# Attention followed by a two-layer feed-forward on one core: the last four loads of v made to wait for an output transpose

## The chip, the cores and the metric

One core of a Trainium2 chip runs the whole kernel. The metric is the device time of one execution in microseconds (us), as a median over runs. The engines are named as the profile names them: PE is TensorE, PEld its weight load, DVE is VectorE, ACT is ScalarE, POOL is GpSimd and SP is SyncE. SPq and POOLq stand for transfers that SP and GpSimd start.

## The reference

```python
def _attn_ref(q, k, v, bias_table):            # q, k, v: 8 batches x 8 heads x 576 x 64
    scores = np.matmul(q, k.transpose(0, 1, 3, 2)) / np.sqrt(D)
    scores = scores + bias[None]               # a bias by distance and head, from 32 buckets
    attn = np.exp(scores - scores.max(-1, keepdims=True))
    attn = attn / (attn.sum(-1, keepdims=True) + 1e-09)
    return np.matmul(attn, v)

def reference(...):
    x = attn_out.transpose(0, 2, 1, 3).reshape(B * S, H * D)   # 4608 x 512
    h = x @ w_in                                                # 512 x 2048
    return np.maximum(0.01 * h, h) @ w_out                      # 2048 x 512
```

## The kernel before

**Attention** runs over 32 pairs of heads: pair n is heads 2p and 2p+1 of batch b, with b = n // 4 and p = n % 4. For each pair the rows of q and k are copied from the loaded tiles `qn` and `kn` into a tile `pr` (L435, DVE), turned by a DMA transpose on SP (`tu<-pr`, L440), and copied into `qt` and `kt` (L466). Scores go to `ps_s` (L492 to L500), the exponentials to `at` (L506 to L513), the bias is multiplied in as a factor (L526), and the product with v goes to `ps_o` and `ps_om` (L547 from the tile `v4`, shown as `v`, and L562 from `vn`). DVE divides by the sums (L574, L575) into `opair`. A DMA transpose on SP (`xT<-opair`, L581) then puts the pair's output into `xT[p]`, where channels are rows and tokens are columns. `xT[p]` is a ring of four batches, 576 columns each, with 64 columns behind the last. One such transpose writes 640 columns, five blocks of 128: the 576 tokens of its batch, and 64 columns past them that carry nothing.

**The feed-forward** takes tiles T of 512 tokens. Its first product reads `xT[0]` to `xT[3]` in turn (L614, later in blocks L671), so a tile can't be finished before the fourth pair of the batch that holds its last token is turned. Its second product is L744, and DVE adds up the results in `y` (L760), which SP stores. The matmuls of the feed-forward stand between those of the attention on the same in-order PE.

**Loads.** v, q and k are loaded by GpSimd, since they change type on the way, in order on one queue. There are two buffers of each, so the load of batch b goes where batch b-2 was. For each b from 2 on, `plan_loads` (L956) queues two loads each for q and k and then `load_v_part` three times (L299): four transfers of `vn` (L302) and two of `v4` (L308). Before its first transfer GpSimd waits until PE has made the last product that reads the old `vn`, that of the fourth pair of batch b-2. Behind the six transfers of v(b) stand on the same queue the four of q and k of batch b+1 (L294), of which the first two serve the first two pairs of that batch.

**The order** of every engine is set before the program runs, by the class `Plan`, which simulates the engines with costs, ranks and tables. In it the load of v for b > 3 is already placed behind the output transpose of the fourth pair of batch b-2 (`avs + xt[...]`, L963). That places the load in the plan alone: the program has no wait of its own for it.

Of the kernel before, what the change touches and what calls it, by code (L numbers as in the profile page):

```python
# [79 lines left out]
class Plan:  # L80
# [32 lines left out]
    def add(self, engine, cost, after, go, rank, take=(), give=(), tail=0.0, at=None):  # L113
        t = {"engine": engine, "cost": cost, "after": list(after), "go": go, "rank": rank, "n": len(self.tasks),
             "take": list(take), "give": list(give), "tail": tail, "end": at, "start": at}
        if at is None:
            self.tasks.append(t)
        return t
# [95 lines left out]
def kernel(  # L214
# [10 lines left out]
    nc = tc.nc  # L225

    B, H, S, D = q.shape
# [5 lines left out]
    n_pairs = H // 2  # L233
# [24 lines left out]
    RING = 4  # L258
    RT = RING * S
    xT = [per.tile([P, RT + P - SL], BF16, name=f"xT{p}") for p in range(n_pairs)]  # L260
# [29 lines left out]
    def load_qk(b, h0, h1, js=(0, 1)):  # L290
        i = b % NBUF
        for j in js:
            src, dst = ((q, qn[i]), (k, kn[i]))[j]
            nc.gpsimd.dma_start(  # L294
                out=dst[0:RQ, h0:h1, :, :].rearrange("r h c d -> r h (c d)"),
                in_=src[b, h0:h1, :, :].rearrange("h (r c) d -> r h (c d)", c=NC),
            )

    def load_v_part(b, j):  # L299
        i = b % NBUF  # L300
        for c in ((0,), (1, 2), (3,))[j]:
            nc.gpsimd.dma_start(  # L302
                out=vn[i][:, c, :, 0:D],
                in_=v[b, :, c * P : (c + 1) * P, :].rearrange("h s d -> s h d"),
            )
        if j == 2:
            for e in range(2):
                nc.gpsimd.dma_start(  # L308
                    out=v4[i][e * SL : (e + 1) * SL, :, e, 0:D],
                    in_=v[b, e::2, NJ * P : S, :].rearrange("h s d -> s h d"),  # L310
                )

    def clear_v(eng, i):
        eng.memset(v4[i], 0.0)
        for e in range(2):
            eng.memset(v4[i][e * SL : (e + 1) * SL, :, e, D : D + 1], 1.0)
        eng.memset(vn[i][:, :, :, D : D + 1], 1.0)
# [452 lines left out]
    rowt, cut, sct, ext, avt, nrt, nmt, xt, vt = {}, {}, {}, {}, {}, {}, {}, {}, {}  # L770
# [19 lines left out]
    def moves(t, work, lane, lead, least, yields=0.39):  # L790
        t["moves"], t["lane"], t["lead"], t["least"], t["yields"] = work, lane, lead, least, yields
        return t

    def pool_load(key, cost, go, work, after=(), rank=1):
        t = add("POOL", cost, prev + list(after), go, rank)
        moves(t, work, 0, min(cost + 1.0, 3.2), cost + 2.2, 0.39 if key[0] in ("qk", "v") else 0.2)
        prev[:] = [t]
        L[key] = t
        return t
# [5 lines left out]
    prev.append(clears[0])  # L805
    pool_load(("qk", 0, 2), 1.4, lambda: load_qk(0, 6, H), 2.0, rank=-9)
    pool_load(("v", 0), 5.2, lambda: [load_v_part(0, j) for j in range(3)], 5.5, rank=-8)
    vt[0] = L["v", 0]
    edges = add("POOL", 1.0, list(prev), lambda: [clear_edges(nc.gpsimd, i) for i in range(3)], -7)
    pool_load(("qk", 1, 0), 1.4, lambda: load_qk(1, 0, 4), 2.6, rank=-4)  # L810
    pool_load(("w_in", 0), 0.8, lambda: load_w_in(0), WH, rank=-4)
    clears.append(add("POOL", 1.2, list(prev), lambda: clear_v(nc.gpsimd, 1), -3))
    prev.append(clears[1])
    vt[1] = pool_load(("v", 1), 5.2, lambda: [load_v_part(1, j) for j in range(3)], VB, rank=-2)
    pool_load(("qk", 1, 1), 1.4, lambda: load_qk(1, 4, H), 2.7, rank=-1)
    pool_load(("w_in", 1), 0.8, lambda: load_w_in(1), WH, rank=6)
# [139 lines left out]
    def plan_loads(b):  # L956
        i = n_pairs * (b - 2)
        for hh in range(2):
            ps = [rowt[i + 2 * hh + x][r] for x in range(2) for r in range(2)]
            pool_load(("qk", b, hh), 1.5, lambda hh=hh: load_qk(b, 4 * hh, 4 * hh + 4), 3.0, ps, 10 * i + 500)  # L960
        avs = [t for p in range(n_pairs) for t in avt[i + p]]
        if b > 3:
            avs = avs + xt[i + n_pairs - 1]  # L963
        vt[b] = pool_load(("v", b), 5.0, lambda: [load_v_part(b, j) for j in range(3)], 5.0, avs, 10 * i + 500)

    oin, ins = {}, {}

# [107 lines left out]
    for n in range(N):  # L1075
        if n >= 2 * n_pairs and n % n_pairs == 0:
            plan_loads(n // n_pairs)
        plan_rows(n)
        if n == 0:
            plan_table()  # L1080
            clears[1]["after"].append(hk4t[1])
        plan_pair(n)
# [47 lines left out]
```

## Time and profile before

| | |
|---|---|
| median of 3 runs | 360.85 us (359.72 to 361.23) |
| the profiled execution | 361.39 us |
| its span, first to last instruction | 359.5 us |
| clock granted to TensorE | 1.0 throughout |
| busy share of the span | PE 98%, DVE 81%, ACT 76%, POOL 19% |

The page of the profile gives busy times by engine and by line, the waits name who held up an engine and how long, the timeline lists instructions by start and duration in us, and the chain is the work that ended last, followed backwards. "To landing" is the time from the issue of a transfer until its data is there. A matmul's end is modelled, so that neighbouring matmuls overlap on paper.

### The profile page before, as it was taken

How to read it: one execution, taken by the hardware profiler on the slowest of the kernel's cores; microseconds unless marked ns; L12 is line 12 of the kernel's file. 1: busy time of each engine (PE TensorE's matmuls, PEld its weight loads, DVE VectorE, ACT ScalarE, POOL GpSimd, SP SyncE). 2: the span in 40 equal slices, each digit the busy share in tenths (PEclk: the TensorE clock that was granted, in tenths of full speed). 3: DMA queues.
4: the chain of work that ended last, by engine and by line, in shares of the span. 5: the costliest groups of instructions: out<-in, count | busy, mean ns of one | idle time of the engine just before them, and what ended most of it. 6: DMA issues, size and time to landing. Idle time of an engine off the chain costs nothing.

```text
span 359.5 us, 10118 instructions
## 1 busy us (share of the span) xinstructions
PE 351.3 (98%) x4204; PEld 256.4 (71%) x4204; DVE 292.8 (81%) x703; ACT 274.4 (76%) x365; POOL 69.3 (19%) x107
## 2 busy tenths in 40 slices
PE   8999999989999999999999999999999999999996
PEld 6666457746577456745677787657888888888885
DVE  6888899785799649976799899999977669578594
ACT  6997998697898899789878788897746656655630
POOL 8956123070005300800260050000000000000000
PEclk9999999999999999999999999999999999999999
DMA  8999999999538993995599999221220011011022
GB/s 125 157 186 194 209 186 110 148 169 190 130 82 96 202 135 83 126 191 66 88 149 139 175 130 130 82 39 47 60 68 2 31 58 61 2 58 60 31 84 93
DMA packets 106941, 39.31 MB, mean 109 GB/s; under 512 B 82320, under 2 KB 105872, under 8 KB 106896
## 3 DMA queue, kind: packets, MB, share of 16 engines
q0 software_dynamic: 53424, 18.21, 49.9%
q1 hardware_dynamic: 53120, 20.03, 31.9%
q8 instruction: 33, 0.54, 0.7%
q10 hardware_dynamic: 352, 0.43, 0.4%
q14 instruction: 12, 0.10, 0.1%
HBM read 36.70 MB, written 9.44 MB: 128 GB/s over the span
## 4 chain that ended last, share of the span: by engine, by line
PE 64%; DMA 14%; DVE 13%; POOL 4%; issue 2%; ACT 1%; DVEq 0%; ACTq 0%; POOLq 0%
PE pm L744 23%; PE pm L614 15%; PE pm L671 12%; PE ps_s L492 5%; DMA w_out_sb<-in_moe_w_out_dram 4%; DMA tu<-pr 4%; PE ps_om L562 3%; DMA xT<-opair 3%; DMA vn<-in_v_dram 3%; PE ps_o L562 3%; DVE sum L712 3%; DVE at L526 3%; DVE opair L575 2%; POOL vn L302 1%; DVE y L760 1%
## 5 line engine op out<-in xcount | busy, mean ns | idle before, releaser
L506 ACT ACTIVATE at<-ps_s 128x1024 bf16<-128x1024 f32 x124 | 120.7, 1033 | 21.2 <-PE ps_s L492 20.4
L614 PE MATMUL pm<-xT,w_in_sb 128*128 128x512 bf16 (+1 forms) x416 | 85.9, 347 | 1.4 <-DMA xT<-opair 1.0
L526 DVE TENSOR_TENSOR at<-at,hk 128x768 bf16<-128x768 bf16 (+4 forms) x156 | 65.7, 448 | 11.5 <-ACT at L506 9.1
L744 PEld LDWEIGHTS <-gt 128*128 128x128 bf16 x576 | 54.4, 98 | 11.7 <-issue 3.4
L614 PEld LDWEIGHTS <-w_in_sb 128*128 128x128 bf16 x416 | 37.7, 98 | 34.1 <-issue 7.1
L690 ACT ACTIVATE gt<-pm 128x512 bf16<-128x512 f32 x88 | 50.9, 627 | 10.4 <-PE pm L614 10.2
L760 DVE TENSOR_TENSOR y<-pm,y 128x512 f32<-128x512 f32 (+1 forms) x53 | 41.1, 776 | 16.1 <-PE pm L744 14.4
L302 POOL DMA_DIRECT2D vn<-in_v_dram x32 | 28.5, 903 | 131.4 <-PE ps_o L562 119.5
L744 PEld LDWEIGHTS <-sum 128*128 128x128 bf16 x432 | 41.2, 98 | 8.1 <-issue 2.1
L562 PEld LDWEIGHTS <-at 128*128 128x128 bf16 x1240 | 41.1, 98 | 2.8 <-issue 0.7
L492 PE MATMUL ps_s<-qt,kt 64*128 64x512 bf16 x256 | 40.0, 382 | 0.2
L744 PE MATMUL pm<-w_out_sb,gt 128*128 128x256 bf16 x288 | 37.9, 273 | 0.0
L744 PE MATMUL pm<-mix,gt 128*128 128x256 bf16 x288 | 36.7, 273 | 0.0
L744 PE MATMUL pm<-w_out_sb,sum 128*128 128x256 bf16 x288 | 36.0, 273 | 0.0
L681 DVE TENSOR_TENSOR at<-pm,at 128x512 f32<-128x512 f32 (+1 forms) x22 | 18.9, 880 | 9.3 <-ACT at L675 7.2
L675 ACT COPY at<-pm 128x1024 f32<-128x1024 f32 x15 | 15.1, 1009 | 13.8 <-PE pm L671 13.8
L562 PE MATMUL ps_o<-vn,at 128*128 128x65 bf16 x640 | 25.2, 193 | 0.1
L562 PE MATMUL ps_om<-vn,at 128*128 128x65 bf16 x600 | 24.1, 194 | 0.0
L513 ACT ACTIVATE at<-ps_s 128x576 bf16<-128x576 f32 x31 | 20.9, 675 | 0.7 <-PE ps_s L500 0.6
L492 PEld LDWEIGHTS <-kt 64*128 64x128 bf16 x256 | 8.2, 94 | 17.4 <-issue 15.3
L508 ACT ACTIVATE at<-ps_s 128x512 bf16<-128x512 f32 x31 | 19.2, 619 | 0.2
L687 ACT ACTIVATE gt<-at 128x1024 bf16<-128x1024 f32 x15 | 15.9, 1057 | 4.0 <-DVE at L681 4.0
(120 smaller groups left out, 526.7 us busy)
## 6 DMA issues: line engine op xcount, KB each, us to landing
out_dram<-y SPq DMA_DIRECT2D x35, 256.0 KB, 2.2
vn<-in_v_dram POOLq DMA_DIRECT2D x32, 128.0 KB, 6.1
qn<-in_q_dram POOLq DMA_DIRECT2D x14, 288.0 KB, 9.9
kn<-in_k_dram POOLq DMA_DIRECT2D x14, 288.0 KB, 11.3
w_in_sb<-in_moe_w_in_dram POOLq DMA_DIRECT2D x2, 1024.0 KB, 11.5
w_out_sb<-in_moe_w_out_dram POOLq DMA_DIRECT2D x2, 1024.0 KB, 17.4
qn<-in_q_dram POOLq DMA_DIRECT2D x4, 144.0 KB, 4.0
v<-in_v_dram POOLq DMA_DIRECT2D x16, 32.0 KB, 6.2
```

The costliest lines, as they stand in the source:

```text
L302: nc.gpsimd.dma_start(out=vn[i][:, c, :, 0:D], in_=v[b, :, c * P : (c + 1) * P, :].rearrange("h s d -> s h d"),)
L492: nc.tensor.matmul(ps[:, e, :], lhsT=kt[r, u * P : (u + 1) * P], rhs=qt[r, 0:512], start=True, stop=True)
L506: nc.scalar.activation(at[:, :, u, 0:512], ps, AF.Exp, scale=scale)
L508: nc.scalar.activation(at[:, :, :, 512:S].rearrange("p e c i -> p c e i"), ps[:, 0, :].rearrange("p (c e i) -> p c e i", e=2, i=SL), AF.Ex ...
L513: nc.scalar.activation(at4[:, 0:S], ps.rearrange("p e i -> p (e i)")[:, 0:S], AF.Exp, scale=scale)
L526: nc.vector.tensor_tensor(out=o, in0=o, in1=m, op=ALU.mult)
L562: nc.tensor.matmul(ps[:, ic, :], lhsT=at[:, o : o + P], rhs=vn[i][:, c, 2 * p + e, :], start=whole and c == 0, stop=not whole and ic == NJ ...
L614: nc.tensor.matmul(pms[T, f][:, o : o + n], lhsT=w_in_sb[:, c, f * P : (f + 1) * P], rhs=xT[c][:, x : x + n], start=(c == 0 and i == 0), s ...
L671: nc.tensor.matmul(ps[:, i, :], lhsT=w, rhs=x, start=fresh and i % 2 == 0 and c == 0, stop=i % 2 == 1 and c == 1, skip_group_check=not fresh)
L690: nc.scalar.activation(gts[T][:, f, :], pms.pop((T, f)), AF.Prelu, bias=0.0, scale=1.0, alpha=0.01)
L744: nc.tensor.matmul(ps[:, ts, :], lhsT=l[:, ts * P : (ts + 1) * P], rhs=r, start=(ts == 0 or apart) and j == 0, stop=(ts == 1 or apart) and ...
L760: nc.vector.tensor_tensor(out=out_, in0=ps, in1=x, op=ALU.add)
```

## The change

For the loads of v for b = 4, 5, 6 and 7, GpSimd first writes a zero into one element of `xT[3]`: row 0, and the first of the 64 columns past batch b-2. The transpose of the fourth pair of batch b-2 writes that column too, so GpSimd has to wait until that transpose has landed. The six transfers of v follow on the same queue.

```diff
+
+    def behind_x(b):
+        o = (b - 2) % RING * S + S
+        nc.gpsimd.memset(xT[n_pairs - 1][0:1, o : o + 1], 0.0)
...
-        vt[b] = pool_load(("v", b), 5.0, lambda: [load_v_part(b, j) for j in range(3)], 5.0, avs, 10 * i + 500)
+        vt[b] = pool_load(("v", b), 5.0, lambda: [behind_x(b) if b > 3 else None, [load_v_part(b, j) for j in range(3)]], 5.0, avs, 10 * i + 500)
```

No instruction of PE, ACT, DVE or SP changes its place. On GpSimd one memset is added ahead of each of the four loads. The first two pieces below stand around the first of these loads, that for b = 4. The first is GpSimd's queue before. `vn_95` and `v_0_97` are the buffers of v, DMASW a semaphore of GpSimd's transfers and DMAHW one of SP's.

```order
L294 DMA kn_93<-in_k_dram 96x4x384 [waits DMASW2_49,DVE_49]
L302 DMA vn_95<-in_v_dram 128x8x64 [waits DMASW3_49,PE_49]
L302 DMA vn_95<-in_v_dram 128x8x64 [waits DMASW4_49,PE_49]
L302 DMA vn_95<-in_v_dram 128x8x64 [waits DMASW5_49,PE_49]
L302 DMA vn_95<-in_v_dram 128x8x64 [waits DMASW6_49,PE_49]
L308 DMA v_0_97<-in_v_dram 64x4x64 [waits DMASW7_49]
L308 DMA v_0_97<-in_v_dram 64x4x64 [waits DMASW0_49]
L294 DMA qn_92<-in_q_dram 96x4x384 [waits DMASW1_49,DVE_49]
```

The same place of GpSimd's queue in the changed kernel; `xT_81` is `xT[3]`.

```order
L294 DMA kn_93<-in_k_dram 96x4x384 [waits DMASW2_49,DVE_49]
L315 MEMSET xT_81 1x1 [waits DMAHW5_49]
L302 DMA vn_95<-in_v_dram 128x8x64 [waits DMASW3_49,PE_49]
L302 DMA vn_95<-in_v_dram 128x8x64 [waits DMASW4_49,PE_49]
L302 DMA vn_95<-in_v_dram 128x8x64 [waits DMASW5_49,PE_49]
L302 DMA vn_95<-in_v_dram 128x8x64 [waits DMASW6_49,PE_49]
L308 DMA v_0_97<-in_v_dram 64x4x64 [waits DMASW7_49]
L308 DMA v_0_97<-in_v_dram 64x4x64 [waits DMASW0_49]
L294 DMA qn_92<-in_q_dram 96x4x384 [waits DMASW1_49,DVE_49]
```

The memset stands ahead of all six transfers and waits for a transfer of SP; everything behind it on the queue follows it. The next output transpose into `xT[3]`, that of pair 15 a batch later, stands so in SP's queue before (L581):

```order
L581 DMA_TRANSPOSE xT_80<-opair 128x5x128 [waits DMAHW5_49,DVE_49]
L440 DMA_TRANSPOSE tu_110<-pr_107 128x12x96 [waits DMAHW6_49,DVE_49]
L440 DMA_TRANSPOSE tu_108<-pr_105 128x12x96 [waits DMAHW0_49,DMAHW7_49,DVE_49,Activation_49]
L581 DMA_TRANSPOSE xT_81<-opair 128x5x128 [waits DVE_49]
L764 DMA out_dram<-y 128x2x256 [waits DMAHW1_49,DVE_49]
```

And so in the changed kernel, where line numbers are four higher:

```order
L585 DMA_TRANSPOSE xT_80<-opair 128x5x128 [waits DMAHW5_49,DVE_49]
L444 DMA_TRANSPOSE tu_110<-pr_107 128x12x96 [waits DMAHW6_49,DVE_49]
L444 DMA_TRANSPOSE tu_108<-pr_105 128x12x96 [waits DMAHW0_49,DMAHW7_49,DVE_49,Activation_49]
L585 DMA_TRANSPOSE xT_81<-opair 128x5x128 [waits DVE_49,Pool_49]
L768 DMA out_dram<-y 128x2x256 [waits DMAHW1_49,DVE_49]
```

SP's instructions keep their places; only the wait for the memset (`Pool_49`) is new.

## The prediction, on record before the changed kernel ran

> **What bounds the kernel now.** The page comes first, for the busy shares, then the waits of PE, since PE is busy nearly throughout.
>
> ```profile
> PE 351.3 (98%) x4204; PEld 256.4 (71%) x4204; DVE 292.8 (81%) x703; ACT 274.4 (76%) x365; POOL 69.3 (19%) x107
> ```
>
> ```profile
> PE pm L614 <- DMA xT<-opair: 1.0, 2, 0.6
> ```
>
> PE is the bound. The second row says how often PE stood still for an output transpose: twice, 1.0 us in all. That is the first yardstick for a change that only frees output transposes. The chain of waits seems to promise more:
>
> ```profile
> 112.73 5.43 DMA xT<-opair
> ...
> 146.96 6.28 DMA xT<-opair
> ```
>
> These are the transposes of pairs 11 and 15, the last of their batches, with the time from issue to landing (second column). The answer on the tile xT has the range for all 24 output transposes (min, median, max):
>
> ```profile
> DMA to landing us min/median/max: 2.6/4.1/14.5
> ```
>
> So both took over twice the shortest. The windows say what PE lost meanwhile (columns: stretch, its length, PE busy):
>
> ```profile
> 111.60:120.00 8.40, 7.80 (x101) 5.18 (x98) 6.79 (x16) 6.06 (x8) 8.14 (x10) 1.00 1.52 150
> ...
> 144.00:156.00 12.00, 11.57 (x136) 7.45 (x133) 11.75 (x33) 9.05 (x13) 7.46 (x10) 1.00 1.54 152
> ```
>
> PE lacks 0.60 us of the first and 0.43 us of the second stretch. The rest of the 5.43 and 6.28 us was covered by other matmuls. The timeline shows the two places, and that a load of v started just ahead of each transpose:
>
> ```profile
> 111.60 3.54 POOL L302 DMA_DIRECT2D vn<-in_v_dram  x4 [32.77 <-PE ps_o L562]
> ...
> 112.73 1.20 SPq L581 DMA_TRANSPOSE xT<-opair  x1
> ...
> 117.23 0.38 PE L614 MATMUL pm<-xT,w_in_sb 128*128 128x512 bf16 x1
> ...
> 118.21 1.24 PE L614 MATMUL pm<-xT,w_in_sb 128*128 128x512 bf16 x5 [0.60 <-DMA xT<-opair]
> ...
> 144.56 3.52 POOL L302 DMA_DIRECT2D vn<-in_v_dram  x4 [24.82 <-PE ps_o L562]
> ...
> 151.61 1.24 PE L614 MATMUL pm<-xT,w_in_sb 128*128 128x512 bf16 x5
> ...
> 153.28 0.38 PE L614 MATMUL pm<-xT,w_in_sb 128*128 128x512 bf16 x1 [0.43 <-DMA xT<-opair]
> ```
>
> **What goes.** The idle column gives 0.60 + 0.43 = 1.03 us. It counts from the modelled end of the matmul before. Counted from start to start, the five matmuls at 151.61 stand (1.24 - 0.38) / 4 = 0.215 us apart. By that pace the matmul at 118.21 would have started at 117.23 + 0.215 = 117.45, which is 0.76 us earlier, and that at 153.28 at 151.61 + 5 x 0.215 = 152.69, 0.59 us earlier. That is 1.35 us. I take 1.2, between the two.
>
> For the stalls to go whole, the transposes must land within 117.45 - 112.73 = 4.72 us and 152.69 - 146.96 = 5.73 us. The median of 4.1, which includes many transposes beside loads, does that; the 2.6 us of the shortest does it easily. So I take both stalls as gone. What is then late next is PE itself, whose matmuls follow one another.
>
> The other two loads have no such stall to give back:
>
> ```profile
> 177.72 3.65 POOL L302 DMA_DIRECT2D vn<-in_v_dram  x4 [25.70 <-PE ps_o L562]
> 178.56 1.23 SPq L581 DMA_TRANSPOSE xT<-opair  x1
> 208.56 3.53 POOL L302 DMA_DIRECT2D vn<-in_v_dram  x4 [22.98 <-PE ps_o L562]
> 209.37 1.29 SPq L581 DMA_TRANSPOSE xT<-opair  x1
> ```
>
> The waits of PE name only the first two places, so nothing is counted for pairs 19 and 23.
>
> **What is added.** Four memsets of one element. The nearest row, GpSimd's small memset, is 0.10 us; the largest that GpSimd makes is 0.60:
>
> ```profile
> 0.24 0.10 POOL L1114 MEMSET const-float32-0.0<- 128x1 f32 x1 [0.24 <-issue]
> ...
> 5.10 0.60 POOL L314 MEMSET v<- 128x520 bf16 x1
> ```
>
> I take 0.10; even 4 x 0.60 = 2.4 us lies on GpSimd, which waits 23 to 33 us ahead of each of these loads (the bracket of the rows above). The waits that the memset gives to later instructions, those of SP and of the DVE instructions that read `xT[3]`, are over long before: the memset at about 116 is followed by the next transpose into `xT[3]` at 146.96.
>
> **What moves.** The start of each load moves from the release by PE to the landing of the transpose. With 2.6 to 4.1 us to landing and 0.1 for the memset, the loads start at 115.4 to 116.9 instead of 111.60, at 149.7 to 151.2 instead of 144.56, at 181.3 to 182.8 instead of 177.72, and at 212.1 to 213.6 instead of 208.56: some 3.5 to 6.6 us later. Behind each stand the loads of q and k on the queue, later by as much. Who waits for them?
>
> v(4) is first used by the product of pair 16, at 149.91, and its last parts were issued at 115.09 and take 6.2 us by the page's median:
>
> ```profile
> 149.91 0.19 PE L547 MATMUL ps_o<-v,at 64*128 64x65 bf16 x1
> ...
> 115.09 1.29 POOL L308 DMA_DIRECT2D v<-in_v_dram  x2
> ```
>
> ```profile
> v<-in_v_dram POOLq DMA_DIRECT2D x16, 32.0 KB, 6.2
> ```
>
> They landed near 123, with 27 us to spare: nothing. The nearest user of the later q and k is at the third place, where the copies for pair 28 need the first loads of batch 7:
>
> ```profile
> 183.58 0.68 POOL L294 DMA_DIRECT2D kn<-in_k_dram  x1
> ...
> 200.12 0.35 DVE L435 COPY pr<-kn 96x768 bf16<-96x768 bf16 x1
> ...
> 203.94 0.69 DVE L760 TENSOR_TENSOR y<-pm,y 128x512 f32<-128x512 f32 x1 [0.81 <-PE pm L744]
> ```
>
> The answers on transfers at 183.58 and 184.90 have these loads of k with their time to landing:
>
> ```profile
> kn<-in_k_dram POOLq DMA_DIRECT2D x1, 288.0 KB, 12.8
> ...
> kn<-in_k_dram POOLq DMA_DIRECT2D x1, 288.0 KB, 16.6
> ```
>
> So k landed at 183.58 + 12.8 = 196.4, and DVE copied it at 200.12: 3.7 us to spare against 3.6 to 5.1 us of delay at this place. At the worst DVE waits 5.1 - 3.7 = 1.4 us, of which the 0.81 us that it idles at 203.94 takes back some; at the best nothing, since the transfers that no longer share the engines with the transpose also go faster. I take 0.2 us. Moving a transfer doesn't shrink it: SP's next transposes (one at 118.21, one at 183.37) share the engines with the load as before, only with a later part of it. Their results are used long after:
>
> ```profile
> 118.21 2.36 SPq L440 DMA_TRANSPOSE tu<-pr  x1
> ...
> 141.65 1.22 ACT L466 COPY kt<-tu 128x576 bf16<-128x576 bf16 x1
> ```
>
> The transpose of 118.21, for pair 18, is copied at 141.65, and pair 17's stands between, so a few us more cost nothing.
>
> **The sum.** The profiled execution took 361.39 us, 1.9 of it around the span of 359.5. Less 1.2, plus 0.2: 360.4. The median is 0.54 below that execution, so the forecast is 360.85 - 1.0 = 359.85 us.
>
> **The rivals.**
>
> *k comes late (slower).* If the first load of k at the third place takes not 12.8 but, as the second one did, 16.6 us, and starts 4.5 us later, it lands 8.3 us later: DVE waits 8.3 - 3.7 = 4.6 us, 0.8 of it in the gap at 203.94. That costs 3.8, less the 1.2 gained: 363.4 us. It turns slower where DVE's wait exceeds 0.8 + 1.2 = 2.0 us, that is, where k is delayed by more than 5.7 us. For it: DMA traffic is heaviest here. Against it: the delay by the rows ends at 5.1. The Trainium skill's page "DMA: Bandwidth & Descriptors", section "Rules for kernel authors", speaks against the change in general: issue a transfer early and wait for it late, so that its fixed cost overlaps with compute. This place, with its 3.7 us, is the only one found where the rows let that rule cost anything.
>
> *No gain.* The transposes could be slow because of SP's own queue: the transpose at 110.18 ahead, stores from 114.30 behind. Then they land as before, the loads only start later, and the time stays 360.85. For it:
>
> ```profile
> 110.18 1.29 SPq L440 DMA_TRANSPOSE tu<-pr  x1
> ...
> 114.30 2.70 SPq L764 DMA_DIRECT2D out_dram<-y  x2
> ```
>
> Against it: at the second place the only store near comes at 148.63, 1.7 us behind the transpose, which was the slower of the two.
>
> *Copies beside GpSimd's issues.* Three copies into `pr` took twice as long as the rest while GpSimd issued a load of v (start, duration):
>
> ```profile
> 179.67 0.35 DVE L435 COPY pr<-qn 96x768 bf16<-96x768 bf16 x1
> 179.94 0.72 DVE L435 COPY pr<-kn 96x768 bf16<-96x768 bf16 x1
> ...
> 210.69 0.71 DVE L435 COPY pr<-kn 96x768 bf16<-96x768 bf16 x1
> 211.58 0.69 DVE L435 COPY pr<-qn 96x768 bf16<-96x768 bf16 x1
> ```
>
> The moved loads leave these copies alone, 3 x 0.35 = 1.05 us of DVE. With the 1.35 us of the stalls at their fullest the time is 360.85 - 2.4 = 358.45. Against it: DVE isn't the bound. The other way round, up to four copies (those at 150.50, 150.77, 154.53 and 154.80) fall into the moved load of the second place; were all doubled and on the path, 360.85 - 1.2 + 1.4 = 361.05. The Trainium skill's page "SBUF — State Buffer", section "Who interferes with whom", has a rule for this: VectorE copies in a two-port mode and GpSimd share a port pair under an exclusive lock, and the later one blocks. It would make the cost real; the doubled rows agree, and this pair of rivals stands for it.
>
> ```profile
> 150.50 0.35 DVE L435 COPY pr<-qn 96x768 bf16<-96x768 bf16 x1
> ```
>
> This one ran while GpSimd issued loads of q and k (149.27 to 152) and was not doubled.
>
> *The chain is right.* If what the chain credits to the two transposes beyond 2 x 2.6 us came off, it would be 5.43 + 6.28 - 5.2 = 6.5 us: 354.3. PE's 7.80 busy of 8.40 us speaks against it.
>
> **How the numbers follow.** Forecast 0.57 (359.3 to 360.5); no gain 0.15; copies freed 0.12; copies newly hit 0.06; k late 0.07; the chain 0.03. The range leaves out the chain and the late k, and ends at 358.4, the freed copies, and at 361.4, the no-gain case with the half us by which medians and single runs differ here: 0.85 or a little more is inside, less some for what I overlooked. About 0.5% (1.8 us) is what a measurement of this kernel can tell from no change. Faster than 359.05: the chain, most of the freed copies, a little of the forecast, 0.16. Slower than 362.65: most of the late k, 0.05. The rest, 0.79, is within.
>
> **What would show it.** Right: PE no longer waits for xT at either place, both transposes land within 4.7 and 5.7 us, each load of v starts behind the landing, and DVE copies k for pair 28 without idling. Wrong: the transposes take 5 us or more with the load held back (no gain), an idle time of DVE ahead of the copies near 200 that ends with a load of k (late k), or a time outside 358.4 to 361.4 with those rows unchanged.

## The result, and the profile after

| | before | changed |
|---|---|---|
| median, 22 runs each | 361.78 us | 360.31 us |
| ratio, 95% interval | | 0.9948 (0.9926 to 0.9971) |
| the profiled execution, its span | 361.39, 359.5 us | 360.92, 359.2 us |

The change makes the kernel faster by 0.5%: 361.78 x 0.0052 = 1.9 us, with an interval of 1.0 to 2.7 us. The ratio leaves out one slow run of the changed kernel, of 366.03 us, and the two medians, over all runs, differ by 1.47 us. The median of before over 22 runs is 0.9 us above that of the three runs that the prediction had.

The waits of PE in the changed kernel hold no wait for an output transpose any more; these are all five rows (columns: us in total, times, the longest). The first row is a wait in the first 20 us, for the first load of v, where the two programs are the same.

```profile
PE ps_o L566 <- DMA vn<-in_v_dram: 1.2, 2, 0.9
PE ps_w L1099 <- DVE junk L331: 1.1, 1, 1.1
PE ps_tx L593 <- DVE opair L579: 0.4, 2, 0.2
PE pm L618 <- DVE opair L579: 0.2, 1, 0.2
PE ps_u L389 <- DVE hk L392: 0.2, 1, 0.2
```

The timeline of the changed kernel at the two places (start, duration; line numbers are four higher than before):

```profile
113.69 1.20 SPq L585 DMA_TRANSPOSE xT<-opair  x1
116.32 0.09 POOL L315 MEMSET xT<- 1x1 bf16 x1 [34.69 <-DMA xT<-opair]
116.83 3.67 POOL L302 DMA_DIRECT2D vn<-in_v_dram  x4 [0.41 <-PE ps_s L496]
117.53 0.59 PE L618 MATMUL pm<-xT,w_in_sb 128*128 128x512 bf16 x2
118.19 1.46 PE L618 MATMUL pm<-xT,w_in_sb 128*128 128x512 bf16 x6
...
147.22 1.20 SPq L585 DMA_TRANSPOSE xT<-opair  x1
149.84 0.09 POOL L315 MEMSET xT<- 1x1 bf16 x1 [24.83 <-DMA xT<-opair]
150.34 3.54 POOL L302 DMA_DIRECT2D vn<-in_v_dram  x4 [0.41 <-PE ps_s L496]
151.82 1.46 PE L618 MATMUL pm<-xT,w_in_sb 128*128 128x512 bf16 x6
```

Each memset starts within 0.1 us of the landing of the transpose (113.69 + 2.58 = 116.27), the load starts 0.4 us after the memset's end, and the six matmuls that read `xT` run without a gap. The answers on xT at 113.69, 147.22, 178.19 and 209.08 have the same landing time for all four transposes:

```profile
DMA to landing us min/median/max: 2.6/2.6/2.6
```

That is as short as the shortest of before, where the two that PE waited for took 5.4 and 6.3 us.

**A yardstick without the start.** The whole spans compare badly, since the first 66 us of the changed kernel's trace ran up to 2.9 us behind that of before, on the same instructions. PE waited 0.9 us for v there (18.59 us), and the granted clock was 0.89 from 15 to 20 us and 0.76 from 20 to 25 us, against 1.00 in the trace of before. It caught up 2.0 us at 71 us, where before waits for a turned row of q and k (`tu`). So I compare the stretch from DVE's first reciprocal of pair 11, ahead of the first held load, to its last of pair 31. The timeline of before:

```profile
110.91 0.18 DVE L574 RECIPROCAL rcp<-ps_om 128x5 f32<-128x5 f32 x1
...
264.44 0.18 DVE L574 RECIPROCAL rcp<-ps_o 128x5 f32<-128x5 f32 x1
```

The timeline of the changed kernel:

```profile
111.87 0.18 DVE L578 RECIPROCAL rcp<-ps_om 128x5 f32<-128x5 f32 x1
...
264.06 0.18 DVE L578 RECIPROCAL rcp<-ps_o 128x5 f32<-128x5 f32 x1
```

That is 153.53 us before and 152.19 after, 1.34 us less, at a granted clock of 1.00 in both. Instruction by instruction the lag is 0.96 us at pair 11, 0.20 us from pair 12 on, and -0.38 us from pair 17 to the end: 0.76 us at the first place, 0.58 us at the second, nothing elsewhere that lasts.

### The profile page after: what moved, and what is told of

It reads as the page before. It is cut to its first block, busy times and chain, and to the rows that moved or that the text cites. A ratio compares the mean times of both kernels' runs of the same rounds, so it can differ in the third digit from the quotient of the medians.

```text
span 359.2 us, 10126 instructions
## 1 busy us (share of the span) xinstructions
PE 352.2 (98%) x4204; PEld 257.1 (72%) x4204; DVE 293.2 (82%) x703; ACT 274.5 (76%) x365; POOL 69.9 (19%) x111
## 4 chain that ended last, share of the span: by engine, by line
PE 89%; DVE 5%; DMA 2%; POOL 2%; issue 1%; ACT 0%; DVEq 0%; POOLq 0%
PE pm L748 30%; PE pm L618 21%; PE pm L675 12%; PE ps_s L496 8%; PE ps_om L566 6%; PE ps_o L566 5%; DMA vn<-in_v_dram 2%; PE ps_s L503 2%; PE ps_s L500 2%; DVE opair L579 1%; PE ps_o L551 1%; DVE sum L716 1%; DVE y L764 1%; POOL vn L302 1%; PE ps_tx L593 1%
## 5 line engine op out<-in xcount | busy, mean ns | idle before, releaser
L566 PEld LDWEIGHTS <-at 128*128 128x128 bf16 x1240 | 42.1, 98 | 3.6 <-issue 1.1
L496 PE MATMUL ps_s<-qt,kt 64*128 64x512 bf16 x256 | 40.2, 383 | 0.2
L566 PE MATMUL ps_o<-vn,at 128*128 128x65 bf16 x640 | 26.0, 194 | 1.4 <-DMA vn<-in_v_dram 1.2
L496 PEld LDWEIGHTS <-kt 64*128 64x128 bf16 x256 | 8.1, 94 | 17.2 <-issue 14.9
```

What stands on the lines that cost most here:

```text
L496: nc.tensor.matmul(ps[:, e, :], lhsT=kt[r, u * P : (u + 1) * P], rhs=qt[r, 0:512], start=True, stop=True)
L566: nc.tensor.matmul(ps[:, ic, :], lhsT=at[:, o : o + P], rhs=vn[i][:, c, 2 * p + e, :], start=whole and c == 0, stop=not whole and ic == NJ ...
```

## The experiments

The stretch of each trace, and what PE lost at the two places, which is the time between the reciprocals around a place, less the same time in the changed kernel (at pair 11 the gap from DVE's second reciprocal to the next one, 7.35 us in the changed kernel; at pair 15 the three gaps from there, 13.93 us):

| kernel | stretch | lost at pair 11 | lost at pair 15 | ratio of times |
|---|---|---|---|---|
| before, first trace | 153.53 | 0.76 | 0.58 | 1 |
| before, second and third trace | 153.90, 153.24 | 0.96, 0.63 | 0.79, 0.42 | |
| all four held (the change), two traces | 152.19, 152.22 | 0, 0 | 0, 0.03 | 0.9948, 0.9943 |
| v(4) held alone | 153.45 | 0 | 1.26 | |
| v(5) held alone | 153.20 | 0.99 | 0 | |
| v(4) and v(5) held, two traces | 152.20, 152.48 | 0, 0 | 0, 0.03 | 0.9967, 0.9982 |
| v(6) and v(7) held | 155.35 | 1.08 | 1.25 | 1.0032 |
| memsets without a wait | 155.40 | 1.33 | 1.07 | 1.0009 |
| loads of v(4) to v(7) left out | 153.47 | 1.26 | 0 | |
| held some 10 us longer | 163.39 | 0 | | 1.0319 |
| held, q and k ahead of v | 152.21 | 0 | 0 | 0.9967 |

The ratios also carry the granted clock, which differs from one execution to the next: in the second run of v(4) and v(5) held, six executions with a mean of 0.995 took 362.78 to 364.41 us, and six with 0.999 or 1.0 took 359.16 to 362.40. The trace of one at 0.995 has a clock of 0.88 from 66 to 80 us, ahead of the first place. By executions of 0.998 and above alone, a choice made after the runs, the medians of the second run of the change, of both runs of v(4) and v(5) held and of q and k ahead of v lie 1.9, 1.7, 1.7 and 1.9 us below that of before beside them, and that of the memsets without a wait 1.3 us above it.

### One half of the change at a time

```diff
-behind_x(b) if b > 3 else None
+behind_x(b) if b == 4 else None
```

> Only the load of v(4) is held back. Measure: the stretch from DVE's first reciprocal of pair 11 to its last of pair 31, 153.53 us before and 152.19 us with the whole change. Theory (two stalls of PE go, 0.76 at pair 11 and 0.59 at pair 15 from start to start): 152.77 us; PE no longer waits for xT at pair 11 and still waits some 0.4 us at pair 15. Rival (the gain comes from the moved loads of the later batches, or from copies of DVE freed there): the stretch stays near 153.5 although the first wait is gone. Rival (SP's own queue makes the transpose slow): it still lands in over 5 us.

The stall at pair 11 was gone (the transpose landed in 2.6 us), that at pair 15 remained. The waits of PE:

```profile
PE pm L618 <- DMA xT<-opair: 1.1, 1, 1.1
```

The stretch, 153.45, missed the 152.77 expected. The first place gave what was expected, but the second lost 1.26 us instead of the 0.58 of the first trace: its transpose took 6.9 us instead of 6.3. So the size of a stall is no constant of the program.

```diff
-behind_x(b) if b > 3 else None
+behind_x(b) if b == 5 else None
```

> Only the load of v(5) is held back. Theory: 153.53 - 0.59 = 152.94 us for the stretch; PE still waits 0.6 us at pair 11 and not at pair 15. A copy of DVE at pair 15's place is doubled by the moved load (0.35 us on DVE, as in the changed kernel) and costs PE nothing. Rival (doubled copies cost time): 153.3 us or more.

Here the stall at pair 15 was gone, and pair 11 lost 0.99 us. The stretch, 153.20, missed the 152.94 expected by 0.26, about what pair 11 lost beyond the 0.76 of the first trace. Each memset removes the stall of its own batch and no other. The two halves act apart.

```diff
-behind_x(b) if b > 3 else None
+behind_x(b) if b > 5 else None
```

> Only the loads of v(6) and v(7) are held back. Theory: nothing for PE, 153.5 us, both waits for xT remain (1.0 us); time as before within its interval. Rival (freed copies of DVE and faster transposes at pairs 19 and 23 bring a part of the gain): 153.2 us or less. Rival (late k at batch 7): 153.9 us or more, with DVE waiting for a load of k ahead of the copies of pair 28.

Both stalls were there, larger than in the first trace of before, and the ratio 1.0032 (0.9994 to 1.0069) shows no gain; the 153.5 us expected for the stretch came out 155.35. The transposes of pairs 19 and 23 landed in 2.6 us and PE had no use for it. What did turn up is the late k. The timeline of DVE in this kernel, ahead of pair 28:

```profile
203.86 0.36 DVE L439 COPY pr<-qn 96x768 bf16<-96x768 bf16 x1
206.63 0.36 DVE L439 COPY pr<-kn 96x768 bf16<-96x768 bf16 x1 [2.41 <-DMA kn<-in_k_dram]
```

The first load of k behind the held v was issued at 190.96 and took 15.6 us, against 12.8 in the trace of before; it landed at 206.6, and DVE waited 2.41 us for it. The gaps between reciprocals from pair 20 to the middle of pair 25 sum to 39.49 us here and 38.70 us in the changed kernel, so of the 2.41 us, 0.79 remained.

### The memset alone

```diff
-        nc.gpsimd.memset(xT[n_pairs - 1][0:1, o : o + 1], 0.0)
+        nc.gpsimd.memset(scrap[0:1, b : b + 1], 0.0)
```

> The four memsets write a tile of their own, so they wait for nothing: the price of four more instructions alone. Theory: 153.5 us for the stretch, loads start as before (0.1 us later), both waits of PE remain; time as before. Rival (it is the pause of GpSimd's queue that a memset makes ahead of a load, not the wait for the transpose): the transposes of pairs 11 and 15 land in under 4 us and the stretch is near 152.2.

The edit also makes a small tile for them, ahead of `xT`:

```diff
+    scrap = per.tile([P, 8], BF16, name="scrap")
```

Without a wait a memset runs as soon as the queue reaches it, long before the load behind it:

```profile
119.79 0.09 POOL L316 MEMSET scrap<- 1x1 bf16 x1
...
144.95 3.52 POOL L303 DMA_DIRECT2D vn<-in_v_dram  x4 [25.07 <-PE ps_o L567]
```

Both stalls remained (2.1 us by the waits of PE), the ratio is 1.0009 (0.9977 to 1.0041). So four memsets without a wait bring nothing, and it is their wait that helps. That they cost nothing isn't shown: the stretch was 155.40 instead of the 153.5 expected, and at a clock of 0.998 and above nine executions have a median of 362.95 us, against 361.65 for fourteen of before. The kernel also has the added tile, and the shortest output transpose of its trace landed in 2.4 us instead of 2.6, so more than the memsets may differ. The run doesn't test a pause just ahead of the load, since none came about. This trace lost another 0.7 us near 188, where ACT waited 2.1 us before it could copy into `y` (L755 before).

### The first two loads held

```diff
-behind_x(b) if b > 3 else None
+behind_x(b) if 3 < b < 6 else None
```

> The loads of v(4) and v(5) are held back, those of v(6) and v(7) not. Theory: the whole gain, 152.2 us for the stretch (153.53 before), and a ratio to before like the change's, 0.995. Rival (the later two loads bring a part): 152.5 us or more.

The stretch was 152.20, the whole gain of the change, and the ratio 0.9967 (0.9937 to 0.9996). A second run of it and one of the change stood beside each other:

> The changed kernel once more, for a second trace and an interval beside the next two. Theory: stretch 152.2 us with no wait of PE for xT, unless the first load of k for batch 7 lands late, as it did with the last two loads held back alone (DVE waited 2.4 us and the stretch from pair 20 to pair 25 lost 0.7 us): then up to 152.9 us. Ratio to before 0.995.

> The loads of v(4) and v(5) held back alone, once more. Theory: stretch 152.2 us, no wait for k at batch 7, since its load isn't held back; ratio as the change's or up to 0.002 lower. Rival (the last two loads bring a part): ratio higher than the change's by more than the intervals.

The change gave 152.22 and 0.9943 (0.9913 to 0.9974), without a wait for k (its trace is of an execution of 365.62 us, with a clock of 0.72 from 75 to 80 us, but of 1.00 in the stretch); the first two alone gave 152.48 and 0.9982 (0.9945 to 1.0019). The 0.26 us of difference lie at pairs 19 to 21, where ACT's copy into `y` came later, by the trace because of another write into `y`. The intervals overlap, and at the clock of 0.998 and above the medians are 360.22 and 360.46, so whether holding the last two loads is worth anything is open. In traces it cost 0.8 us once (the late k) and spared 0.3 us once.

### The load of v left out

```diff
-[load_v_part(b, j) for j in range(3)]
+[load_v_part(b, j) for j in range(3) if b < 4]
```

> The loads of v for batches 4 to 7 are left out, and no memset is made, so the output is that of old values of v; all else is done. Theory (the load of v beside it makes the output transpose slow): the transposes of pairs 11 and 15 land in 2.6 to 3.5 us, both waits of PE go, the stretch is near 152.2 us, since no other wait of PE hangs on the loads. Rival (SP's own queue makes them slow): 5 us or more, stretch near 153.5. Rival (loads cost time elsewhere too): under 151.9 us.

The landing times expected, 2.6 to 3.5 us, were missed at both places, and the sign named for SP's queue came instead: over 5 us, and a stretch of 153.47. The stall at pair 15 was gone, that at pair 11 was not (1.26 us). GpSimd's queue tells why: with v gone the loads behind it moved up, and a load of q and k now ran beside the transpose.

```profile
100.14 0.67 POOL L294 DMA_DIRECT2D qn<-in_q_dram  x1 [10.28 <-DVE pr L439]
100.80 0.67 POOL L294 DMA_DIRECT2D kn<-in_k_dram  x1
110.92 0.95 POOL L294 DMA_DIRECT2D qn<-in_q_dram  x1 [9.45 <-DVE at L530]
111.87 0.68 POOL L294 DMA_DIRECT2D kn<-in_k_dram  x1
144.97 1.06 POOL L294 DMA_DIRECT2D qn<-in_q_dram  x1 [32.42 <-DVE pr L439]
146.02 0.67 POOL L294 DMA_DIRECT2D kn<-in_k_dram  x1
157.23 0.67 POOL L294 DMA_DIRECT2D qn<-in_q_dram  x1 [10.54 <-DVE pr L439]
```

The transposes at 114.26 and 149.00, 3.3 and 4.0 us behind the issue of such a load, took 5.9 and 5.4 us. The second was still slow; it was just within the 5.73 us that the prediction worked out for PE not to wait. The transposes of pairs 19 and 23 had no load near:

```profile
177.49 2.21 SPq L444 DMA_TRANSPOSE tu<-pr  x1
179.80 1.22 SPq L585 DMA_TRANSPOSE xT<-opair  x1
182.97 0.37 SPq L768 DMA_DIRECT2D out_dram<-y  x1
...
209.26 1.29 SPq L444 DMA_TRANSPOSE tu<-pr  x1
210.82 1.32 SPq L585 DMA_TRANSPOSE xT<-opair  x1
```

They landed in 2.6 and 2.7 us, against 4.6 and 6.7 us in the trace of before, although SP's own queue had the same transpose ahead and the same store behind. So loads of q and k by GpSimd beside it make the transpose slow too, and SP's queue alone doesn't. This rests on one trace.

### Held much longer

```diff
-        nc.gpsimd.memset(xT[n_pairs - 1][0:1, o : o + 1], 0.0)
+        for _ in range(60):
+            nc.gpsimd.memset(xT[n_pairs - 1][0:1, o : o + 1], 0.0)
```

> Each memset is made 60 times, which holds the loads some 5 us longer at 0.09 us each. Theory with the late k of the prediction: q and k of the next batch land 5 us later still; at the third place k had 3.7 us to spare before and lost about 3 to the change, so DVE waits some 3 to 5 us for k ahead of the copies of pair 28, 0.8 us of which is covered: stretch 154 to 156 us, slower than the changed kernel by 2 to 4 us. Rival (more slack than the rows say, or backlog that catches up): 152.2 us as in the changed kernel.

Sixty memsets of one element took 10 to 12 us, not 5, so the hold was twice as long as meant. DVE then waited for q and k at three places, in its timeline:

```profile
136.55 0.36 DVE L440 COPY pr<-qn 96x768 bf16<-96x768 bf16 x1 [2.65 <-DMA qn<-in_q_dram]
137.86 0.36 DVE L440 COPY pr<-kn 96x768 bf16<-96x768 bf16 x1 [0.95 <-DMA kn<-in_k_dram]
...
174.57 0.36 DVE L440 COPY pr<-qn 96x768 bf16<-96x768 bf16 x1 [6.26 <-DMA qn<-in_q_dram]
176.05 0.35 DVE L440 COPY pr<-kn 96x768 bf16<-96x768 bf16 x1 [1.12 <-DMA kn<-in_k_dram]
...
210.09 0.36 DVE L440 COPY pr<-qn 96x768 bf16<-96x768 bf16 x1 [2.94 <-DMA qn<-in_q_dram]
211.37 0.36 DVE L440 COPY pr<-kn 96x768 bf16<-96x768 bf16 x1 [0.92 <-DMA kn<-in_k_dram]
```

The ratio is 1.0319 (1.0264 to 1.0374), the stretch 11.2 us longer than with the change. The price of holding is real and comes by q and k, as the prediction had it for the third place. With so long a hold the first two places pay too. Not all of the 11.2 us is waiting: at the second place PE stood still for 4.9 us, and the granted clock was 0.50 from 175 to 180 us and 0.85 from 180 to 185 us.

### q and k ahead of v

```diff
-lambda hh=hh: load_qk(b, 4 * hh, 4 * hh + 4)
+lambda hh=hh: [load_v_part(b - 1, j) for j in range(3)] if hh == 0 and b > 4 else load_qk(b, 4 * hh, 4 * hh + 4)
...
-[behind_x(b) if b > 3 else None, [load_v_part(b, j) for j in range(3)]]
+[behind_x(b) if b > 3 else None, load_qk(b + 1, 0, 4) if 3 < b < B - 1 else [load_v_part(b, j) for j in range(3)]]
```

> All four holds, but on GpSimd's queue the first loads of q and k of the next batch stand ahead of the six transfers of v, right behind the memset, for batches 5, 6 and 7. v has some 27 us to spare, k 3.7. Theory: the transposes still land in 2.6 us and both waits of PE go; the first load of k is issued about as early as before the change, so it can't be late; stretch 152.2 us in any state of the transfers, ratio at or below the change's, 0.993 to 0.995. Rival (v now lands late, or q and k ahead slow the turned rows): 152.6 us or more.

The stretch was 152.21, and nobody waited for k or v. But DVE waited at another place:

```profile
171.35 0.36 DVE L439 COPY pr<-qn 96x768 bf16<-96x768 bf16 x1 [2.07 <-DMA tu<-pr]
```

That wait was made up for by pair 19. The ratio, 0.9967 (0.9933 to 1.0001), missed the 0.993 to 0.995 expected; with the clock of 0.998 and above the median is that of the change, 360.23 against 360.22. No version here beats the change by more than the intervals.

### How large is a stall?

> The kernel before, unchanged, for a second trace. Where a load of v was not held back in the other runs, PE lost 0.76 to 1.33 us at pair 11 and 0.58 to 1.26 us at pair 15 (against the kernels that hold it back), and the one trace of before is the lowest at both. If that spread is from one execution to the next, this trace shows stalls anywhere in it and a stretch of 153.5 to 154.8 us; if the first trace is typical of this program, 153.5.

> A third trace of the kernel before, for the same question: a stretch of 153.5 to 154.8 us, the mean of the three above 153.9 if the first was a low one.

The kernel before lost 0.96 and 0.79 us in its second trace and 0.63 and 0.42 us in its third, so the first was in the middle. The mean of the three stretches is 153.56 us, below the 153.9 that would have made the first a low one, and 1.35 above the change's two. The larger stalls of the edited kernels (up to 1.33 and 1.26 us) did not show in three traces of before. Why they are larger is open. The kernels that hold v(4) alone, v(5) alone or the last two, and that with memsets alone, were traced on one chip, and the second and third trace of before on another, so the chip and the edit aren't told apart. The medians of before beside them, 361.65 and 361.70 us at a clock of 0.998 and above, give no sign of a slower chip.

## Why the prediction was right, and where it was off

**The step that carried it held.** The transposes beside the load were slow because of the load, and without it they landed in 2.6 us; both stalls of PE went, and nothing at PE took their place. The edits that hold v(4) or v(5) alone show it one place at a time.

**The size from start to start was the right one.** The prediction worked out 0.76 and 0.59 us that way, and 1.03 us in all from the idle column, and took 1.2 between. The trace gave 0.76 and 0.58. The idle column, which counts from the modelled end of the matmul before, gave 0.60 and 0.43 and is too low.

**The 0.2 us for a late k was not paid in the two traces of the change.** DVE copied k for pair 28 without idling:

```profile
199.50 0.35 DVE L439 COPY pr<-qn 96x768 bf16<-96x768 bf16 x1
199.77 0.35 DVE L439 COPY pr<-kn 96x768 bf16<-96x768 bf16 x1
200.04 0.35 DVE L439 COPY pr<-qn 96x768 bf16<-96x768 bf16 x1
```

The first load of k was issued 3.2 us later than before (186.78 against 183.58) and took 10.9 us instead of 12.8, so it landed at 197.6, with 2.1 us to spare; in the second trace of the change it landed at 203.6 and was copied at 204.4. So the margin is thin: with v(6) and v(7) held alone it was overdrawn by 2.4 us. The rival named the right place and mechanism. The rows didn't bear out that traffic is heaviest at that place: the DMA share before is 1.50 from 177 to 189 us, 1.54 from 144 to 156 and 1.60 from 208 to 220. Its price came out smaller: the prediction let 0.8 us of a wait be covered, and of 2.41 us, 1.6 were.

**The sum was low.** Forecast 1.0 us, measured 1.9 (1.0 to 2.7) and in the second run of the change 362.59 x 0.0057 = 2.1. The traces explain 1.35. The other half microsecond lies within the intervals; stalls larger than in the traces of before, such as five of the edited kernels' traces showed, would account for it, but that isn't shown. The clock doesn't: at 0.998 and above, 360.22 us stand against 362.14, still 1.9 us. The forecast of 359.85 us came out 0.46 below the median of 360.31. That is in part luck: it started from a median of before that was 0.9 us too low, and its gain was too small, and the two errors partly offset each other.

**The rival that there is no gain** fell with the landing times: 2.6 us at all four places, with SP's queue unchanged.

**Copies beside GpSimd's issues** happened both ways, and no loss or gain at PE came of it. The timeline of the changed kernel:

```profile
150.70 0.69 DVE L439 COPY pr<-qn 96x768 bf16<-96x768 bf16 x1
151.32 0.34 DVE L439 COPY pr<-kn 96x768 bf16<-96x768 bf16 x1
...
179.29 0.35 DVE L439 COPY pr<-qn 96x768 bf16<-96x768 bf16 x1
179.56 0.35 DVE L439 COPY pr<-kn 96x768 bf16<-96x768 bf16 x1
```

The copy at 150.70 doubled when the load of v moved onto it, and that at 179.56 went back to 0.35 us when the load moved off. The Trainium skill's page "SBUF — State Buffer", section "Who interferes with whom", says that VectorE in a two-port mode and GpSimd exclude each other from a shared port pair, the later one being blocked. The trace agrees for that copy, but the next one, at 151.32, ran in 0.34 us although the load's issue went on to 153.88. DVE's lag grew by 0.35 us at pair 16 and was gone by pair 17, since PE didn't wait for it.

**The chain** promised 6.5 us, and the stretch shows a fifth of that. It names what released each step, not what the step would have cost without the wait.

The Trainium skill's page "DMA: Bandwidth & Descriptors", section "Rules for kernel authors", says to issue a transfer early and to wait for it late. Here that is borne out only where the later transfer has a user near: a hold of 4 to 6 us was free, one of some 14 us cost 3%, a lower clock included.

## What to carry to other kernels

A bulk load that has tens of microseconds to spare should not start just ahead of a short transfer that the bound engine waits for; here a one-element write that depends on the short transfer was enough to order them. Before holding it back, look at what is queued behind it and how long that can wait: here v could wait 27 us, and the k behind it 3.7. And read what such a stall is worth from the bound engine, from start to start, in more than one trace, and look at the granted clock of each execution before comparing times.

## What the runs showed that was not expected

- The same transpose took 5.3 to 6.9 us beside a load by GpSimd, in all traces at these two places, and 2.6 us without: the load more than doubles it. Loads of q and k did the same as loads of v (5.9 and 5.4 us).
- A one-element memset takes 0.09 us alone, but sixty to the same element took 10.2, 12.0, 9.8 and 11.4 us, 0.16 to 0.20 us each.
- Between the end of a memset that waited and the first load behind it lie 0.4 us in which GpSimd is idle. The rows put this down to a matmul of L496, which isn't the product that the load waits for; what it is isn't shown. The prediction had only the 0.1 us of the memset here.
